# First weights in pieces by pairs of column blocks, and the state of the first batch added on VectorE

## The chip, the cores and the metric

The kernel runs on one core of a Trainium2 chip. A core has a matrix engine (TensorE, PE in the profile, PEld for its weight loads), VectorE (DVE), ScalarE (ACT), GpSimd (POOL) and SyncE (SP), which here issues all transfers. Each engine takes its instructions in the order in which the program gives them. The metric is the device time of one execution in microseconds; the median of three runs is shown.

## The reference

Two stages. The first is an mLSTM cell over 4 batches, 8 heads, 768 steps, head width 40, with a matrix state C per head; the second mixes the result (4 x 768 x 320) by a Fourier transform over tokens and features and puts it through a two-layer MLP with 320 -> 1280 -> 320.

```python
for t in range(S):
    m_new = np.maximum(f_gate[:, :, t] + m, i_gate[:, :, t])
    f_stab = np.exp(f_gate[:, :, t] + m - m_new)
    i_stab = np.exp(i_gate[:, :, t] - m_new)
    C = f_stab[:, :, None, None] * C + i_stab[:, :, None, None] * np.einsum('bhd,bhe->bhde', vt, kt)
    n = f_stab[:, :, None] * n + i_stab[:, :, None] * kt
    h_tilde = np.einsum('bhde,bhe->bhd', C, qt)
    y[:, :, t] = o * h_tilde / denom
...
X = np.real(np.fft.fft(np.fft.fft(x, axis=1), axis=2))
u = x + X
un = (u - mu) / np.sqrt(var + 1e-06)
ch = np.maximum(un @ w_ch1, 0.0) @ w_ch2
return u + ch
```

The weights `w_ch1` and `w_ch2` come as 64-bit floats and are turned into 32-bit floats on the chip.

## The kernel before

**Tiling.** The 768 steps of a batch are 6 chunks of 128 tokens (`NT`). Within a chunk the cell is matrix work: scores q.k (`ps`, L465), weighing by the gates' exponentials (`W`, L421 on ScalarE, L471 on VectorE), the part from the state (`ph<-qg,C`, L479), the part from the chunk itself (`ph<-W,kvt`, L486), and the chunk's contribution to the state (`pc<-vw,kvt`, L496). Then `h` is copied out by ScalarE, transposed (`px`, L535) and divided (L544 to L550, VectorE). Three buffers `C_bufs` hold the state in turn.

**State.** In batches 1 to 3 GpSimd multiplies the old state by its decay into the next buffer (L455), and VectorE adds `pc` to it (L515; a copy, L513, for chunk 0). In batch 0 GpSimd writes the decayed state into a side buffer `Cd`, two multiplications by an identity add it to `pc` on TensorE (L501), and ScalarE copies the sum into the next state (L511).

**Mixing and MLP.** The Fourier stage folds token blocks on VectorE and GpSimd (`mix_fold`), multiplies by tables (`pz`, `pzt`, then `pu`), adds to x (`mix_add`, L743 to L757, VectorE), centres (`uc`, L765, ScalarE), transposes (`put`, L772) and copies out (`uT`, L777, ScalarE). The MLP works on two groups of three token blocks; 1280 hidden columns are 10 blocks, taken as 5 pairs. For batch 0, `mlp_in` (L837 and, for the 64 odd features, L841) gives a pair's two banks, which ScalarE puts through a relu (L850), and `mlp_out` (L943) multiplies by the second weights. For the other batches, `mlp_block` and `mlp_out_pair` use sums of blocks (seven products in place of eight), which `weight_sums`, `mlp_sums`, `hidden_sums` and `out_weight_sums` make on VectorE.

**Weights in pieces.** A `Piece` is 128 x 640 64-bit numbers, 640 KB. It is loaded into one of two `raw` buffers (L334), taken apart by two VectorE instructions (`take`, L344 and L346), converted by two of ScalarE (`convert`, L351 and L352) and joined by three of VectorE (`join`, L358 to L364). The first weights are five pieces: the first half of the columns of features 0 to 127, the same half of the last 128 features, the 64 features between (`w1t_sb`), then the second halves. So a first product needs three pieces. The second weights are five pieces more, one for each pair.

**The order** is written out by hand. `at(slot, phase, fn)` puts a call into a plan, and the plan is run in the order of (slot, phase); that order is the order in each engine's queue. Batch 0 has slots 0 to 21 for its chunks (three slots each), 18 to 31 for the mixing, and 31 on for its MLP, one product step a slot; chunks of batch 1 start at slot 32 and lie between these. `EVAC`, `FILL`, `MAIN`, `FILL_PE` are phases 0 to 3. `when` gives the slots of take, convert and join of each piece, `early` and the loop under it the slots of its load. A load waits for its `raw` buffer to be free, and everything behind it in SyncE's queue waits with it.

Steps in slots 31 to 37 that are spoken of below, in the order of ScalarE's queue: exponentials of batch 1's chunk 0, first half (slot 32), relu of the first pair (33, phase 0), exponentials, second half (33), centring of token block 4 (33), copy of its transpose (34), conversion of the first piece of the second weights (34), relu of the second pair (35). On VectorE: addition for block 4 (31), join of the last first-weight piece (32), taking (33), weighing of chunk 0 (34), addition for block 2 (35), join (35), state copies (36), taking (36), addition for block 3 (37).

## Time and profile before

| | |
|---|---|
| median of three runs | 420.96 us (420.94 to 421.48) |
| the profiled execution | 420.94 us |
| its span, first to last instruction | 419.2 us |
| mean granted TensorE clock | 0.999 |
| bytes moved | 47.14 MB, mean 112 GB/s |
| first products of the MLP of batch 0 | from 58.0 us |
| first products with the second weights | from 122.6 us |

A row of the timeline is: start and duration in us, engine, line of the kernel, operation, output<-inputs, shapes, count, and in brackets the engine's idle time before it with what ended it. Rows of consecutive instructions of one line are merged, so the duration of a row with x4 is that of all four. In the page's second part a digit is the busy share in tenths of one of 40 slices of the span (10.5 us each).

### The profile page before, as it was taken

Reading aid. Unit: us, or ns where it says so; the run is one execution under the profiler, and the core shown is the slowest. Engines: PE = TensorE matmul, PEld = TensorE weight load, DVE = VectorE, ACT = ScalarE, POOL = GpSimd, SP = SyncE. Lnnn points to the kernel's source line nnn. Section 1 sums busy time; section 2 is a strip of 40 time slices with the busy share of each in tenths; the row PEclk is TensorE's granted clock in tenths of the full one; section 3 lists DMA queues with packets and bytes.
Section 4 is the critical chain, followed back from the end, with each engine's and each line's share of the span. In section 5 each row is a group of like instructions: output and inputs, shape, how many; then the busy total and the mean of one; then the engine's idle time right before and its main releaser. Section 6 shows DMA issues by size and latency. Waiting matters only on the chain.

```text
span 419.2 us, 8001 instructions
## 1 busy us (share of the span) xinstructions
PE 408.1 (97%) x2966; PEld 302.4 (72%) x2966; DVE 288.8 (69%) x682; ACT 189.5 (45%) x493; POOL 112.9 (27%) x194
## 2 busy tenths in 40 slices
PE   8999999999999999999999999999999999999997
PEld 6877555566567778776549998976559988455996
DVE  8789895777895638777765569788663786335652
ACT  6986376686561222654455413744451113355000
POOL 5554201468431520442231430351220000020000
PEclk9999999999999999999999999999999999999999
DMA  7899297567765254276100554310000000000010
GB/s 230 288 250 318 71 278 257 185 162 219 236 189 164 59 155 139 64 210 197 50 0 2 156 149 131 100 42 1 0 2 0 33 31 34 0 2 0 16 48 31
DMA packets 20549, 47.14 MB, mean 112 GB/s; under 512 B 2784, under 2 KB 9312, under 8 KB 20384
## 3 DMA queue, kind: packets, MB, share of 16 engines
q1 hardware_dynamic: 20512, 46.65, 36.7%
q8 instruction: 23, 0.38, 0.4%
q14 instruction: 14, 0.11, 0.1%
HBM read 42.52 MB, written 4.11 MB: 111 GB/s over the span
## 4 chain that ended last, share of the span: by engine, by line
PE 82%; DVE 7%; DMA 4%; issue 3%; ACT 2%; POOL 1%; ACTq 0%; DVEq 0%; POOLq 0%; SPq 0%
PE po L999 18%; PE pm L897 17%; PE po L943 8%; PE pm L902 5%; PE ps L465 5%; PE ph L486 4%; PE pu L729 4%; PE ph L479 3%; PE pm L837 3%; DMA raw<-in_w 3%; PE px L535 2%; PE put L772 2%; PE pz L698 2%; DMA kvt<-in_kv 1%; PE pz L686 1%
## 5 line engine op out<-in xcount | busy, mean ns | idle before, releaser
L949 DVE SCALAR_TENSOR_TENSOR x<-po,rstd,x 128x160 f32<-128x160 f32 (+1 forms) x69 | 27.0, 395 | 40.2 <-PE po L999 34.1
L906 DVE TENSOR_TENSOR h<-h,pm 128x384 f32<-128x384 f32 x60 | 30.5, 550 | 30.5 <-ACT h L919 20.9
L421 ACT ACTIVATE W<-W,colT 128x128 f32<-128x128 f32 x144 | 45.0, 395 | 0.0
L443 POOL TENSOR_SCALAR_AFFINE_SELECT W<-W 128x1024 f32<-128x1024 f32 x18 | 21.6, 1198 | 81.0 <-ACT W L421 59.1
L943 PE MATMUL po<-w_sb,h 128*128 128x320 f32 x120 | 34.4, 435 | 0.0
L897 PE MATMUL pm<-uT,w_sb 128*128 128x384 f32 x90 | 32.8, 492 | 0.2 <-DVE uT L885 0.2
L471 DVE TENSOR_TENSOR W<-ps,W 128x512 f32<-128x512 f32 x48 | 30.7, 680 | 2.6 <-POOL W L443 2.4
L837 PE MATMUL pm<-uT,w_sb 128*128 128x384 f32 x80 | 29.6, 499 | 0.7 <-DVE x L749 0.5
L777 ACT COPY uT<-put 128x384 f32<-128x384 f32 x24 | 11.2, 478 | 40.2 <-PE put L772 40.2
L943 PEld LDWEIGHTS po<-w_sb,h 128*128 128x128 f32 x120 | 22.2, 190 | 9.5 <-issue 0.8
L999 PE MATMUL po<-T,S 128*128 128x160 f32 x180 | 27.9, 302 | 0.6 <-DVE x L949 0.6
L465 PE MATMUL ps<-qk 40*128 40x128 f32 x384 | 27.8, 284 | 0.0
L999 PEld LDWEIGHTS po<-T,S 128*128 128x128 f32 x180 | 25.5, 190 | 2.2 <-DVE x L949 1.0
L792 POOL TENSOR_TENSOR t<-rstd 128x6 f32<-128x6 f32 x12 | 2.9, 244 | 89.2 <-DVE v L790 88.6
L999 PE MATMUL po<-w_sb,h 128*128 128x160 f32 x180 | 26.4, 301 | 0.0
L465 PEld LDWEIGHTS ps<-qk 40*128 40x128 f32 x384 | 23.4, 187 | 4.1 <-issue 0.7
L999 PEld LDWEIGHTS po<-w_sb,h 128*128 128x128 f32 x180 | 25.1, 190 | 1.3 <-DVE x L949 0.3
L486 PE MATMUL ph<-W,kvt 128*41 128x128 f32 x384 | 25.8, 277 | 0.0
L431 POOL TENSOR_TENSOR qg<-qk,Gb 128x512 f32<-128x512 f32 x18 | 25.2, 1402 | 0.1
L524 ACT COPY h<-ph 41x512 f32<-41x512 f32 (+1 forms) x16 | 9.3, 583 | 34.9 <-PE ph L486 34.8
L479 PEld LDWEIGHTS ph<-qg,C 128*128 128x128 f32 x160 | 20.0, 191 | 6.3 <-issue 2.5
L897 PEld LDWEIGHTS pm<-uT,w_sb 128*128 128x128 f32 x90 | 16.2, 190 | 10.8 <-DVE h L906 1.5
(207 smaller groups left out, 864.6 us busy)
## 6 DMA issues: line engine op xcount, KB each, us to landing
W<-M_d SPq DMA_DIRECT2D x18, 512.0 KB
kvt<-in_kv SPq DMA_DIRECT2D x24, 324.0 KB
qk<-in_qkT SPq DMA_DIRECT2D x48, 160.0 KB
raw<-in_w SPq DMA_DIRECT2D x10, 640.0 KB
Gb<-G_d SPq DMA_DIRECT2D x36, 128.0 KB
so<-in_o SPq DMA_DIRECT2D x24, 160.0 KB
out<-x SPq DMA_DIRECT2D x24, 160.0 KB
ds_sb<-in_dft_s SPq DMA_DIRECT2D x1, 1155.0 KB
```

Of the source, the lines that this page charges most:

```text
L421: nc.scalar.activation(out=k.W[:, h, :], in_=M, func=AF.Exp, scale=-1.0, bias=colT[:, c, 0, b * H + h:b * H + h + 1])
L431: nc.gpsimd.tensor_tensor(out=k.qg, in0=k.qk[:, 0], in1=k.Gb, op=OP.mult)
L465: nc.tensor.matmul(k.ps[hip][:, p, :], k.qk[r, 1, p, :], k.qk[r, 0, p, :], start=True, stop=True)
L471: nc.vector.tensor_tensor(out=Wv, in0=k.ps[hip], in1=Wv, op=OP.mult)
L479: nc.tensor.matmul(k.ph[:, p, :], k.C[:, p, :], k.qg[:, p, :], start=(p == 0), stop=False, skip_group_check=True)
L486: nc.tensor.matmul(k.ph[hip * 64:hip * 64 + D1, p, :], k.v1[:, 2 * p + hip, :], k.W[:, 2 * p + hip, :], start=(c == 0 and p == 0), stop=Tr ...
L837: nc.tensor.matmul(k.pm[i], w1_sb[:, ch, f0:f0 + L], u[2 * ch], start=(ch == 0), stop=False)
L897: nc.tensor.matmul(bank, w, u, start=start, stop=True, skip_group_check=True)
L906: nc.vector.tensor_tensor(out=h, in0=h, in1=bank, op=OP.add)
L943: nc.tensor.matmul(k.po, hidden(gr, f)[:, i * L:(i + 1) * L], w2_sb[:, f, :], start=(f == 0), stop=(f == NFF - 1))
L949: nc.vector.scalar_tensor_tensor(out=u, in0=po, scalar=k.rstd[:, c:c + 1], in1=u, op0=OP.mult, op1=OP.add)
L999: nc.tensor.matmul(po, a[:, f], w[:, f], start=start and f == 0, stop=f == half - 1, skip_group_check=True)
```

## The change

It has two parts, and two small ones that follow from them.

- The first weights lie in `w1_sb` as five groups, one for each pair of column blocks, of five 128-column blocks: features 0 to 127 for either block of the pair, the last 128 features for either, and the 64 features between. One piece is one group. `w1t_sb` is gone; the host packs the array accordingly, and the products and weight sums read the new places.
- The slots of the pieces change: the second piece is loaded at slot 6 and converted in slots 11 to 22, and so on; the last piece of the first weights has slots 31, 32 and 33, and the pieces of the second weights start one slot later.
- In batch 0 the state is handled as in the other batches: GpSimd writes the decayed state into the next buffer, VectorE adds `pc` (or copies it, chunk 0). The identity multiplications and ScalarE's copies are gone, and so are the `Cd` buffers and their clearing.
- The name of the change also speaks of sums for the first pair of token blocks; the diff has no line on `hidden_sums` or its slots.

```diff
+    w1_sb = const.tile([L, NFF // 2, 5, L], FP, name="w1_sb")
-    w1_sb = const.tile([L, 2, DFF], FP, name="w1_sb")
-    w1t_sb = const.tile([L, DFF // 2], FP, name="w1t_sb")
...
         mlstm_load(0, 2)
-        w1_pieces[1].load()
-        for t in hT_bufs + Cd_bufs:
+        for t in hT_bufs:
             nc.gpsimd.memset(t, 0.0)
...
-    w1_pieces = [Piece([w1_sb[:, f // 2, f % 2 * part:(f % 2 + 1) * part]], w_ch1[:, f * part:(f + 1) * part])
-                 for f in (0, 2, 1, 3)]
-    w1_pieces.insert(2, Piece([w1t_sb], w_ch1[:, 4 * part:]))
+    w1_pieces = [Piece([w1_sb[:, i].rearrange("p k t -> p (k t)")], w_ch1[:, i * 5 * L:(i + 1) * 5 * L])
+                 for i in range(NFF // 2)]
...
-                nc.gpsimd.tensor_tensor(out=k.Cd[r] if b == 0 else k.C_next[r, :, m], in0=k.C[r, :, m], in1=d,
-                                        op=OP.mult)
+                nc.gpsimd.tensor_tensor(out=k.C_next[r, :, m], in0=k.C[r, :, m], in1=d, op=OP.mult)
...
-            if add:
-                for hip in range(2):
-                    r = slice(hip * 64, hip * 64 + D)
-                    nc.tensor.matmul(k.pc[r], ident[:, r], k.Cd, start=False, stop=True, skip_group_check=True)
...
-                if b == 0:
-                    nc.scalar.copy(out=Cv, in_=k.pc[r])
-                elif c == 0:
+                if c == 0:
                     nc.vector.tensor_copy(out=Cv, in_=k.pc[r])
                 else:
                     nc.vector.tensor_tensor(out=Cv, in0=Cv, in1=k.pc[r], op=OP.add)
...
-            nc.tensor.matmul(k.pm[i], w1_sb[:, ch, f0:f0 + L], u[2 * ch], start=(ch == 0), stop=False)
+            nc.tensor.matmul(k.pm[i], w1_sb[:, f // 2, 2 * ch + i], u[2 * ch], start=(ch == 0), stop=False)
...
-    when = [((2, 0.7), (4, 0.5), (6, 0.6)), ((6, 0.7), (7, 0.5), (8, 0.6)), ((11, 0.7), (13, 0.5), (22, 0.6))]
-    when += [((22, 0.7), (23, 0.7), (27, 0.6)), ((27, 0.7), (28, 0.7), (32, 0.6))]
-    when += [((s, 0.7), (s + 1, 0.7), (s + 2, 0.6)) for s in (33, 36, 39, 42, 45)]
+    when = [((2, 0.7), (4, 0.5), (6, 0.6)), ((11, 0.7), (13, 0.5), (22, 0.6)), ((22, 0.7), (23, 0.7), (27, 0.6)),
+            ((27, 0.7), (28, 0.7), (31, 0.6))]
+    when += [((s, 0.7), (s + 1, 0.7), (s + 2, 0.6)) for s in (31, 34, 37, 40, 43, 46)]
     pieces = w1_pieces + w2_pieces
     for n, (w, p) in enumerate(zip(when, pieces)):
-        if n > 4:
+        if n > 3:
             at(when[n - 2][2][0] + 1, FILL + 0.7, p.load)
...
-             (5, mlstm_load_decay, 4), (6, None, 2), (7, mlstm_load_o, 3), (7, mlstm_load, 5),
-             (11, mlstm_load_decay, 5), (11, None, 3), (11, mlstm_load_o, 4), (12, load_tables, None),
-             (14, mlstm_load_o, 5), (23, None, 4)]
+             (5, mlstm_load_decay, 4), (6, None, 1), (7, mlstm_load_o, 3), (7, mlstm_load, 5),
+             (11, mlstm_load_decay, 5), (11, None, 2), (11, mlstm_load_o, 4), (12, load_tables, None),
+             (14, mlstm_load_o, 5), (23, None, 3)]
```

## The prediction

> **What bounds the kernel now.** I read the page first (busy shares, then the slices), then the chain of waits, then the timeline of each engine from 0 to 130 us, where all that the change touches lies, and last the busy time by windows around the one long wait found there. The page:

> ```profile
> PE 408.1 (97%) x2966; PEld 302.4 (72%) x2966; DVE 288.8 (69%) x682; ACT 189.5 (45%) x493; POOL 112.9 (27%) x194
> DMA  7899297567765254276100554310000000000010
> ```

> TensorE is busy for 97% of the span, so what it is made to wait anywhere is paid in full, and other work counts only where TensorE comes to wait for it. The transfers fill the first 120 us and are thin after that. The first batch, up to 58 us, from the timelines of TensorE, ScalarE and VectorE (start, duration, instruction, count, idle time before it and its releaser):

> ```profile
> 15.77 0.60 ACT L511 COPY C<-pc 40x164 f32<-40x164 f32 x2 [0.19 <-PE pc L496]
> 16.14 0.44 PE L297 MATMUL pd<-dec,spread_sb 32*128 32x80 f32 x2 [0.42 <-DVE dec L293]
> 21.91 0.45 PE L501 MATMUL pc<-s_last,ident 128*40 128x164 f32 x4
> 22.41 0.62 ACT L511 COPY C<-pc 40x164 f32<-40x164 f32 x2 [0.80 <-PE pc L501]
> 23.76 0.66 PE L535 MATMUL px<-ident,h 128*128 128x128 f32 x4 [0.41 <-ACT h L528]
> 39.00 1.28 DVE L471 TENSOR_TENSOR W<-ps,W 128x512 f32<-128x512 f32 x2
> 39.35 0.61 ACT L511 COPY C<-pc 40x164 f32<-40x164 f32 x2 [0.63 <-PE pc L501]
> 40.07 1.13 PE L479 MATMUL ph<-qg,C 128*128 128x128 f32 x8 [0.82 <-POOL eo L618]
> ```

> The state C of each chunk goes through ScalarE; at 40.07 TensorE waits for it (the copies end at 39.96, which fits better than the releaser named). VectorE is full from 24.8 to 41.3 us and has only 0.33 us of idle time up to 51.8. Then the first MLP. Same columns, from SyncE's, ScalarE's, VectorE's and TensorE's timelines, and one line by windows (busy time of the engines, granted clock, DMA share, GB/s):

> ```profile
> 59.91 0.53 SPq L334 DMA_DIRECT2D raw<-in_w  x1
> 60.35 1.26 ACT L421 ACTIVATE W<-W,colT 128x128 f32<-128x128 f32 x4
> 61.72 0.87 ACT L850 ACTIVATE h<-pm 128x384 f32<-128x384 f32 x2
> 62.48 1.27 ACT L421 ACTIVATE W<-W,colT 128x128 f32<-128x128 f32 x4
> 63.65 0.61 ACT L765 ACTIVATE uc<-x 128x384 f32<-128x384 f32 x1
> 64.56 0.49 PE L772 MATMUL put<-ident,uc 128*128 128x128 f32 x3
> 67.83 0.49 DVE L344 TENSOR_SCALAR e<-raw 128x640 uint32<-128x640 uint32 x1 [5.02 <-DMA raw<-in_w]
> 68.35 0.83 ACT L351 ACTIVATE e<-e,ebias 128x640 uint32<-128x640 uint32 x1 [2.79 <-DVE e L344]
> 73.60 0.69 DVE L513 COPY C<-pc 40x164 f32<-40x164 f32 x2 [0.23 <-PE pc L496]
> 76.58 2.82 PE L837 MATMUL pm<-uT,w_sb 128*128 128x384 f32 x8 [0.52 <-DVE x L749]
> 64.00:66.00 2.00, 2.00 (x10) 1.06 (x10) 0.00 (x0) 0.73 (x2) 1.62 (x2) 1.00 1.07 284
> ```

> The weight piece asked for at 59.91 lands only at 67.8, behind saturated transfers (share 1.00 to 1.07 from 58 to 68 us). VectorE waits 5.02 us for it; ScalarE reaches its conversion with all of TensorE's near work (relu, exponentials, centring for the transpose at 64.56) already done, so nothing is lost. That order is what the change turns round.

> **The change, part by part.** All sums are made in the profiled execution: 420.94 us, of which 419.2 is the span; the median shown is 420.96.

> *Layout of the first weights and of its sums.* The same matmuls, tails and four weight sums of 128x640 read other offsets; nothing. The words "sums for the first pair of token blocks" have no line in the diff; nothing.

> *State of the first batch.* Gone are 16 identity matmuls (21.91 to the next at 22.30, so 0.39 us per chunk, four chunks, 1.6 us), ten copies on ScalarE (0.30 each) and two small memsets on GpSimd, 0.23 each, hidden beside the gate scans. The decay on GpSimd writes the next state instead of the side buffer, same shape and count (0.46). Added on VectorE are ten instructions, priced by the later batches' rows of the same form, 0.69 us a pair for a copy (L513) and 0.68 for an add (L515). What is queued behind them decides:
> - Chunk 0: VectorE now has to wait for pc (15.72) and copy C (15.77 to 16.45) before qg (L429, 0.60) and dec (0.2). dec ends at 17.3, so pd, which started at 16.14, starts at 17.3: +1.15 us on TensorE.
> - Chunks 1 to 3: per chunk TensorE saves those 0.39 us and, for two of them, the 0.41 wait for h, which ScalarE now copies first. So +1.15 becomes +0.15 at the state product of chunk 2 (one wait more is used up by C), -0.8 at chunk 3 and -1.2 at chunk 4.
> - VectorE, meanwhile, can't use the early piece that was taken out of slots 6 to 8 (0.9 taking, 3.3 joining): the add of chunk 2 stands before the weighing of chunk 3 and waits for pc at about 27.9, so that weighing starts at 28.6 instead of 28.16, +0.45. From there its queue is full as before, with one add before the weighing of chunk 4 (0.68; the taking of a piece at 31.0, 1.45 beside GpSimd's qg, may be 0.3 shorter: +0.85 altogether) and one behind the weighing of chunk 5 (0.67). C of chunk 5 is ready at 39.00 + 0.85 + 1.28 - 0.08 + 0.67 = 41.7 us, and TensorE's state product starts at 41.72 instead of 40.07.
> Result: **+1.65 us** at the end of the first batch, because the folds and divisions behind it are on VectorE as well. From both sides: -2.4 (1.6 of matmuls and two waits of 0.4, if VectorE has the room) and +2.5 (1.15 + 0.69 + 0.67, if nothing is won back). I take the walk through the queues.

> *The pieces of the first weights.* Before, five pieces were converted in slots 2-6, 6-8, 11-22, 22-27 and 27-32. After: 2-6, 11-22, 22-27, 27-31, 31-33. The load of 640 KB at 7.95 us goes; the next three keep their places in SyncE's queue with other contents. The fifth piece is asked for where the first piece of the second weights was, at slot 28, into a buffer free at 57.5, behind the same loads: 59.91, landed at 67.8. But its conversion stands at slot 32, ahead of relu, exponentials and centring. So ScalarE, done with the first four exponentials at 61.6, stands until VectorE has taken the piece, and converts from 68.35 to 69.8. Queued behind it: two relu, four exponentials and the centring of token block 4, which take 63.65 - 61.72 = 1.93 to reach the centring, from 69.72. That starts at 71.65 and ends at 72.26; the transpose on TensorE follows at 72.3 instead of 64.56. TensorE is done with the two products ahead of it at 64.65, and all behind the transpose waits in order: **+7.65 us**. The bounds are 6.5 (a landing 1.2 us sooner, as 655 KB less went before at 280 GB/s would save half of 2.3) and 8.5 (0.85 for the relu again, if the exponentials behind them wait). What the cover was worth: the same 5.02 us wait cost nothing while only the second weights hung on it.

> *The second weights, one slot later.* Joining the first of their pieces moves from before the state copies at 73.60 to between these and block 3's addition (L743 to L757), where only a taking of 0.93 stood. The join is 0.79 + 0.82 + 0.83 with overlaps, 2.35. TensorE's product at 76.58 waits for L749 already (0.52 idle), so 2.35 - 0.93 = **+1.4 us**; bounds 0, if VectorE is ahead after the stall, and 2.3, when GpSimd's work makes it longer as at 24.82 (1.83 for 0.8). The waits for weights at 96 and 106 us move behind the weighings: from -0.8 (idle 0.23 and 0.61 gone) to +0.8 (a join of 2.4 in the place of a take and a wait of 1.15), I take 0.

> *The clock after an idle TensorE.* No idle time over 1.25 us is in this trace, and the granted clock is 1.00 in every window, so no row prices a gap of 7.6. Nearest is the start, where the first six idle products took 2.93 us, against 0.60 for two at 54.96: 2.93 - 3 x 0.60 = 1.1 us of slow products. From below 0 (below nothing makes no sense, for a product can't become faster than at full clock), from above 2.9, if all that stretch's time is added. I take **+1.1**, by the row it is nearest to.
> [...]

> Sum: 420.94 + 1.65 + 7.65 + 1.4 + 1.1 = **432.7 us**.

> **Rivals.**
> - *No stall, and the first batch gains.* It decides at one point: does the fifth piece land before ScalarE is through the exponentials at 61.6? Then 420.94 - 2.4 = 418.5, faster. For it: the transfers' share is 0.21 from 42 to 48 us and one early load is gone. Against: from the asking to 61.6 are 1.7 us, where the same place in the queue took 7.9.
> - *The stall, but a shorter first batch.* VectorE squeezes the adds into its gaps: -2.4 + 7.65 + 1.4 gives 427.6. For it: four waits of 0.4 to 0.8 on TensorE before 44 us hang on ScalarE, which is relieved. Against: VectorE has no gap from 24.8 on.
> - *No stall, but VectorE the bound of the first batch:* 1.65 + 1.4, 424.0. The same landing decides.
> - *The change doesn't do what it says:* for the sums of the first pair this holds, and it gives the forecast's time.

> **How the numbers follow.** Forecast 0.62, stall with a shorter first batch 0.24, no stall but a loss 0.07, no stall and a gain 0.07. The forecast's own range is 429.5 to 436.5 (clock and stall at their ends); for 8 in 10 I reach down to 427.3, which takes in most of the second case. Within 0.2%, 0.84 us, is about what can't be told from no change: faster 0.06, same 0.02, slower 0.92.

> **What would show it.** ScalarE's first conversion line (L351 before) after 60 us should have an idle time of about 6.7 us before it, and TensorE's next transpose one of about 7.6 after ScalarE's centring, with a granted clock under 1.00 in the next slice if the clock falls. The state product of chunk 5 should start near 41.7, pd near 17.3, and the first MLP product near 59.6. The prediction falls if the fifth piece is taken before 63, or if that transpose has no wait.

## The result, and the profile after

The changed kernel takes 442.73 us (median of 4 runs, 441.49 to 445.02) against 421.22 us (4 runs, 420.94 to 422.31) for the kernel before in the same comparison: a ratio of 1.051 [1.046, 1.057], some 21.5 us slower. The forecast was 432.7 with a range to 436.5, so the direction held and the size did not. The profiled execution took 445.02 us, the slowest of the four, with a span of 443.3 us, 24.1 more than before; the sums below are made in it.

First the page of the kernel after: busy times, and the granted clock by slices.

```profile
PE 417.7 (94%) x2950; PEld 309.2 (70%) x2950; DVE 290.5 (66%) x692; ACT 186.6 (42%) x483; POOL 113.3 (26%) x192
PEclk9898997779998999999999999999999999999999
```

TensorE is busy for 9.6 us longer than before (408.1) with 16 matmuls fewer, and its clock, 9 in every slice before, dips in six slices, all in the first 145 us. So there are two kinds of loss to look for: time in which TensorE stands, and time in which it runs slowly. The timeline of TensorE has both (start, duration, instruction, idle time before it and its releaser):

```profile
16.88 0.45 PE L294 MATMUL pd<-dec,spread_sb 32*128 32x80 f32 x2 [1.67 <-DVE dec L290]
20.15 1.85 PE L471 MATMUL ph<-qg,C 128*128 128x128 f32 x8
43.40 1.13 PE L471 MATMUL ph<-qg,C 128*128 128x128 f32 x8 [0.94 <-DVE C L500]
61.34 2.85 PE L821 MATMUL pm<-uT,w_sb 128*128 128x384 f32 x8
76.83 0.90 PE L757 MATMUL put<-ident,uc 128*128 128x128 f32 x3 [8.77 <-ACT uc L750]
80.52 2.51 PE L714 MATMUL pu<-dd_sb,Z 128*128 128x321 f32 x4
84.22 2.20 PE L821 MATMUL pm<-uT,w_sb 128*128 128x384 f32 x6
94.14 5.46 PE L821 MATMUL pm<-uT,w_sb 128*128 128x384 f32 x8 [2.79 <-DVE x L734]
120.67 1.16 PE L471 MATMUL ph<-qg,C 128*128 128x128 f32 x8 [0.97 <-POOL qg L426]
132.46 1.13 PE L471 MATMUL ph<-qg,C 128*128 128x128 f32 x8 [1.60 <-DVE x L535]
146.69 3.50 PE L927 MATMUL po<-w_sb,h 128*128 128x320 f32 x12
```

The row at 76.83 is the stall that was foretold: the transpose of token block 4 waits 8.77 us for ScalarE's centring. The rows behind it show what was not foretold in its size: the same four products of `pu` take 2.51 us at 80.52, where they took 1.35, and the eight of `pm` at 94.14 take 5.46 in place of 2.82. The same rows in the kernel before (those at 64.56 and 76.58 stand in the prediction):

```profile
58.00 2.85 PE L837 MATMUL pm<-uT,w_sb 128*128 128x384 f32 x8
66.47 1.35 PE L729 MATMUL pu<-dd_sb,Z 128*128 128x321 f32 x4
68.93 2.22 PE L837 MATMUL pm<-uT,w_sb 128*128 128x384 f32 x6
99.44 1.16 PE L479 MATMUL ph<-qg,C 128*128 128x128 f32 x8 [0.23 <-POOL qg L431]
110.20 1.13 PE L479 MATMUL ph<-qg,C 128*128 128x128 f32 x8 [0.61 <-DVE den L544]
122.60 5.65 PE L943 MATMUL po<-w_sb,h 128*128 128x320 f32 x20
```

Laid side by side, stretch by stretch:

| TensorE, from and to | before | after | more |
|---|---|---|---|
| start to the first MLP product | 58.00 | 61.34 | 3.34 |
| to the transpose of block 4 | 6.56 | 15.49 | 8.93 |
| to the products behind `pu` (84.22) | 4.37 | 7.39 | 3.02 |
| to the products that wait for block 3's addition (94.14) | 7.65 | 9.92 | 2.27 |
| to the state product at 120.67 | 22.86 | 26.53 | 3.67 |
| to the state product at 132.46 | 10.76 | 11.79 | 1.03 |
| to the first product with the second weights | 12.40 | 14.23 | 1.83 |
| to the end of the span | 296.6 | 296.6 | 0.0 |

The sum is 24.1 us: all of it is lost before the second weights are used. The cause of the stall stands in the timelines of SyncE, VectorE and ScalarE:

```profile
63.60 0.53 SPq L331 DMA_DIRECT2D raw<-in_w  x1
72.37 0.49 DVE L341 TENSOR_SCALAR e<-raw 128x640 uint32<-128x640 uint32 x1 [6.23 <-DMA raw<-in_w]
72.90 0.83 ACT L348 ACTIVATE e<-e,ebias 128x640 uint32<-128x640 uint32 x1 [7.95 <-DVE e L341]
74.26 0.85 ACT L834 ACTIVATE h<-pm 128x384 f32<-128x384 f32 x2
75.00 1.27 ACT L416 ACTIVATE W<-W,colT 128x128 f32<-128x128 f32 x4
76.17 0.61 ACT L750 ACTIVATE uc<-x 128x384 f32<-128x384 f32 x1
```

The fifth piece is asked for at 63.60 and taken at 72.37. ScalarE stands 7.95 us in front of its conversion, and the relu, the exponentials and the centring (76.17), for which the data had long been there, come only after it. The windows (busy time of TensorE, weight load, VectorE, ScalarE and GpSimd, then the granted clock, DMA share, GB/s) tell when the clock fell and rose again:

```profile
18.00:20.00 2.00, 2.00 (x21) 1.71 (x19) 0.80 (x2) 1.98 (x9) 1.64 (x6) 0.56 0.82 270
20.00:22.00 2.00, 2.00 (x13) 1.73 (x10) 1.68 (x3) 0.21 (x1) 0.00 (x0) 0.59 1.00 211
...
72.00:74.00 2.00, 0.00 (x0) 0.00 (x0) 1.14 (x3) 1.10 (x2) 0.00 (x0) 0.71 0.32 130
...
80.00:82.00 2.00, 2.00 (x5) 1.08 (x4) 0.00 (x0) 1.38 (x5) 0.00 (x0) 0.50 0.70 194
82.00:84.00 2.00, 2.00 (x8) 1.00 (x7) 0.00 (x0) 2.00 (x6) 0.00 (x0) 0.73 0.04 8
```

From about 72.8 to 83.1 the array ran at half its clock (0.50 in each window of 2 us from 74 to 82), more than six microseconds of that with TensorE at work. The same shows from 93.3 to 100.1 (0.50 from 94 to 100), and for 3.4 us each at 18.2, 38.7 and 134.3 (0.50 in windows that lie within them: 18.5 to 21.5, 40 to 42, 134.5 to 137.5).

### The profile page after: what moved, and what is told of

Read it like the earlier page. It is cut to its first block, busy times and chain, and to the rows that moved or that the text cites. A ratio compares the mean times of both kernels' runs of the same rounds, so it can differ in the third digit from the quotient of the medians.

```text
span 443.3 us, 7963 instructions
## 1 busy us (share of the span) xinstructions
PE 417.7 (94%) x2950; PEld 309.2 (70%) x2950; DVE 290.5 (66%) x692; ACT 186.6 (42%) x483; POOL 113.3 (26%) x192
## 4 chain that ended last, share of the span: by engine, by line
PE 80%; DVE 12%; ACT 2%; DMA 2%; issue 2%; POOL 2%; ACTq 0%; DVEq 0%; POOLq 0%
PE po L983 17%; PE pm L881 16%; PE po L927 7%; PE pm L886 5%; PE ph L478 5%; PE ps L457 5%; PE ph L471 4%; PE pu L714 4%; PE pm L821 3%; DMA raw<-in_w 2%; PE put L757 2%; PE px L520 2%; PE pz L683 2%; PE pc L487 1%; PE pz L671 1%
## 5 line engine op out<-in xcount | busy, mean ns | idle before, releaser
L438 POOL TENSOR_SCALAR_AFFINE_SELECT W<-W 128x1024 f32<-128x1024 f32 x18 | 21.5, 1192 | 98.3 <-ACT W L416 74.3
L821 PE MATMUL pm<-uT,w_sb 128*128 128x384 f32 x80 | 33.1, 547 | 2.9 <-DVE x L734 2.8
L881 PE MATMUL pm<-uT,w_sb 128*128 128x384 f32 x90 | 32.8, 492 | 0.2 <-DVE uT L869 0.2
L457 PE MATMUL ps<-qk 40*128 40x128 f32 x384 | 28.8, 286 | 0.6 <-PE pM L215 0.4
L983 PE MATMUL po<-T,S 128*128 128x160 f32 x180 | 27.9, 302 | 0.6 <-DVE x L933 0.6
L457 PEld LDWEIGHTS ps<-qk 40*128 40x128 f32 x384 | 24.1, 189 | 4.9 <-issue 1.6
L478 PE MATMUL ph<-W,kvt 128*41 128x128 f32 x384 | 27.5, 289 | 0.0
L471 PEld LDWEIGHTS ph<-qg,C 128*128 128x128 f32 x160 | 21.2, 202 | 8.2 <-issue 3.9
L500 DVE TENSOR_TENSOR C<-C,pc 40x164 f32<-40x164 f32 x32 | 10.3, 322 | 25.3 <-PE pc L487 23.3
L471 PE MATMUL ph<-qg,C 128*128 128x128 f32 x160 | 23.1, 291 | 3.5 <-DVE x L535 1.6
```

The costliest lines, as they stand in the source:

```text
L457: nc.tensor.matmul(k.ps[hip][:, p, :], k.qk[r, 1, p, :], k.qk[r, 0, p, :], start=True, stop=True)
L471: nc.tensor.matmul(k.ph[:, p, :], k.C[:, p, :], k.qg[:, p, :], start=(p == 0), stop=False, skip_group_check=True)
L478: nc.tensor.matmul(k.ph[hip * 64:hip * 64 + D1, p, :], k.v1[:, 2 * p + hip, :], k.W[:, 2 * p + hip, :], start=(c == 0 and p == 0), stop=Tr ...
L821: nc.tensor.matmul(k.pm[i], w1_sb[:, f // 2, 2 * ch + i], u[2 * ch], start=(ch == 0), stop=False)
L881: nc.tensor.matmul(bank, w, u, start=start, stop=True, skip_group_check=True)
L983: nc.tensor.matmul(po, a[:, f], w[:, f], start=start and f == 0, stop=f == half - 1, skip_group_check=True)
```

## The experiments

Two theories stood at the start. **The order**: the fifth piece's conversion stands ahead of ScalarE's near work, and all else follows from that wait. **The layout, the transfers or the state**: the new pieces, or VectorE's additions, cost the time in themselves. Each kernel was timed against the kernel before on the same chip. The table has one profile of each as well: `pm - ps` is the time from the scores of chunk 0 to the first MLP product, which leaves out the start (the scores began between 6.89 and 9.64 us in these profiles). The last column lists the stretches at half clock up to 150 us, as start and length. A stretch's length is worked out from windows of 2 us: the sum of (1 - clock) x 2 x 2 us, for a window that lies wholly in a stretch shows a clock of 0.50. A profile is of one run: those of x9, x10 and x11 are of the slowest run of their kernel (428.88, 428.93 and 426.90 us), that of x8 of the fastest.

| kernel | median us | ratio to before | pm - ps | half clock: start (length) |
|---|---|---|---|---|
| before | 421.22 | | 50.45 | none |
| after | 442.73 | 1.051 [1.046, 1.057] | 54.30 | 18.2 (3.4), 38.7 (3.4), 72.8 (10.2), 93.3 (6.8), 134.3 (3.4) |
| x1_fifth_later | 425.30 | 1.009 [1.006, 1.012] | 52.70 | 37.7 (3.4) |
| x2_state_alone | 426.92 | 1.013 [1.008, 1.018] | 54.93 | 43.9 (3.4) |
| x3_pieces_alone | 440.54 | 1.042 [1.037, 1.048] | 50.45 | 68.0 (10.2), 88.5 (6.8), 129.4 (3.4) |
| x7_pieces_later | 422.62 | 1.001 [1.000, 1.003] | 50.36 | none |
| x6_filled_18 | 440.04 | 1.042 [1.041, 1.044] | 52.62 | 37.8 (3.4), 89.0 (6.8), 130.0 (3.4) |
| x4_filled | 448.92 | 1.063 [1.055, 1.071] | 54.34 | 18.3 (3.4), 38.8 (3.4), 96.8 (6.8), 137.8 (3.4) |
| x8_own_buffer | 436.24 | 1.033 [1.031, 1.035] | 54.32 | 18.5 (3.4), 39.0 (3.4) |
| x5_qg_first | 425.74 | 1.009 [1.007, 1.011] | 51.13 | 37.7 (3.4) |
| x9_take_sooner | 425.66 | 1.010 [1.007, 1.013] | 55.04 | 45.0 (3.4) |
| x10_sooner_qg_first | 425.35 | 1.008 [1.006, 1.010] | 56.31 | 31.4 (6.8), 45.0 (3.4) |
| x11_early_load | 423.91 | 1.004 [1.002, 1.006] | 51.23 | 35.5 (3.4), 114.0 (6.8) |
| x12_order | 427.40 | 1.012 [1.009, 1.014] | 52.62 | 41.6 (6.8), 109.9 (3.4) |

### The pieces at their old places in the queues

```diff
-    when += [((s, 0.7), (s + 1, 0.7), (s + 2, 0.6)) for s in (31, 34, 37, 40, 43, 46)]
+    when += [((s, 0.7), (s + 1, 0.7), (s + 2, 0.6)) for s in (33, 36, 39, 42, 45, 48)]
```

> The changed kernel, but the fifth piece of the first weights is taken, converted and joined in slots 33, 34 and 35, behind the relu and the centring of token block 4, and the second weights in slots 36 to 50. Theory 'order in ScalarE's queue': the wait of 8.77 us at the transpose goes, and with it the 2.79 us wait at the following pair and the slow clock behind both, so 424 us, which is before plus the 3.3 us by which the first batch ends later (423 to 426). Rival 'state': the loss is that of the first batch and of a clock that falls there and does not recover; then this stays above 432 us.

From 1.051 to 1.009: the places in the queues, of the fifth piece and of those of the second weights, and nothing else, are worth 18 of the 21.5 us ((1.0512 - 1.0087) x 421.2). The transpose of block 4 has no wait in this profile, and the clock does not fall behind it; ScalarE still waits for the piece, but behind its centring (rows of ScalarE and TensorE):

```profile
66.44 0.60 ACT L750 ACTIVATE uc<-x 128x384 f32<-128x384 f32 x1
67.34 0.49 PE L757 MATMUL put<-ident,uc 128*128 128x128 f32 x3
71.07 0.83 ACT L348 ACTIVATE e<-e,ebias 128x640 uint32<-128x640 uint32 x1 [2.71 <-DVE e L341]
```

That settles the order as the main cause.

### One part of the change at a time

`x2_state_alone` is the kernel before with the state added by VectorE; `x3_pieces_alone` is the change with the old way of the state (identity matmuls, ScalarE's copies).

> The kernel before with only the state of the first batch moved to VectorE; pieces and slots as before. Theory 'order in ScalarE's queue': the first product of the MLP starts 1.7 to 3.5 us later, nothing else moves, 422.5 to 424.5 us. Rival 'state': above 430 us.

> The changed kernel with the state of the first batch as before (identity products on TensorE, copies on ScalarE). Theory 'order in ScalarE's queue': the transpose waits 8 to 9 us as in the changed kernel, the clock falls behind it; the first batch ends at 58 us or up to 2 us sooner, as a piece is out of its VectorE queue; 436 to 440 us. Rival 'state': below 430 us.

The pieces alone give 440.54, the state alone 426.92, both more than expected: 19.1 and 5.5 us over the 421.43 of their comparison, more together than the 21.5 of the whole change, so the parts do not simply add up. In x2's profile the product of chunk 5's state waits 2.15 us for VectorE's addition, where it waited 0.82:

```profile
43.30 1.47 PE L475 MATMUL ph<-qg,C 128*128 128x128 f32 x8 [2.15 <-DVE C L504]
```

Last, x3 with the edit of x1:

> The pieces by pairs alone (state as before), with the fifth in slots 33 to 35. Theory 'order in ScalarE's queue': with the conversion behind the centring nothing is left of the loss, 420.5 to 422 us, the same as before. Rival 'a piece more among the first products costs by itself' (VectorE 3.4 us, ScalarE 1.5 us, a slot later for the second weights): 424 us or more.

422.62 against 422.10, 1.001 [1.000, 1.003]. So the layout, the packing and the later asking for the second piece cost nothing that can be measured. What x1 still loses is the state's.

### Idle time or clock: the stall filled with products

A row of idle products, whose output nothing reads, is put into TensorE's queue ahead of the transpose of block 4; they fill the wait without shortening it. The fill was meant for about 8 us.

```diff
+    def idle_more(n):
+        pw = ps_h.tile([L, 2 * L], FP, name="pi", tag="ph")
+        for i in range(n):
+            nc.tensor.matmul(pw, rest[:, 0:L], rest, start=True, stop=True, skip_group_check=True)
+
+    at(33, FILL_PE + 4.9, idle_more, 36)
```

> The changed kernel with 36 products of zeros put on TensorE ahead of the transpose that waits, about 7.7 us of work that nothing reads. If the idle time itself costs clock: the transpose starts at the same time or at most 0.5 us later, the granted clock stays at 1.00 from 68 to 84 us and the products behind it take their full-clock times, so 438 to 440 us, 3 us less than the changed kernel. If the low clock has another cause: 442 to 444 us, and the clock still falls near 73 us.

One call is two instructions in the trace and takes 0.44 us, so 36 of them took 15.7 us, twice what was meant, and the transpose was late by them (83.50). The time of this run says little; its clock says more, 1.00 in every window from 68 to 96. With 18 calls the fill ends where the wait did:

> The changed kernel with 18 products of zeros ahead of the waiting transpose, half of x4's, 7.8 us. Idle time costs clock: the transpose starts within 0.3 us of the time at which ScalarE has centred, the clock stays at 1.00 up to the next gap, the stretch from the transpose to the additions of block 2 takes 4.4 us in place of 7.4, so 438 to 440.5 us. If not: 442 to 444 us.

Two rows of x6's timeline, the fill and the transpose behind it, and the next gap:

```profile
67.33 7.93 PE L1108 MATMUL pi<-rest 128*128 128x256 f32 x36
75.39 0.55 PE L757 MATMUL put<-ident,uc 128*128 128x128 f32 x3
...
89.74 5.46 PE L821 MATMUL pm<-uT,w_sb 128*128 128x384 f32 x8 [2.80 <-DVE x L734]
```

From the transpose to the products behind `pu` it is 4.43 us (75.39 to 79.82), nearly as before the change (4.37), against 7.39 in the kernel after. So the wait itself costs its length, and its being idle costs 3.0 us more; the ratio goes from 1.051 to 1.042, with intervals that do not meet. Behind the unfilled gap of 2.80 at 89.74 the clock still halves (0.50 in the windows from 90 to 94): 5.46 in place of 2.82.

### Landing or place in the queue: a buffer of its own for the fifth piece

The order of the change is kept, but the fifth piece is loaded at slot 23 into a free part of the hidden layer's buffer.

```diff
-            self.raw = cp.tile([L, n], mybir.dt.int64, name="raw", tag="raw")
+            if self is w1_pieces[4]:
+                self.raw = hid[1, 1][:, 0:2 * n].bitcast(mybir.dt.int64)
+            else:
+                self.raw = cp.tile([L, n], mybir.dt.int64, name="raw", tag="raw")
...
-            at(when[n - 2][2][0] + 1, FILL + 0.7, p.load)
+            at(*((23, FILL + 0.9) if n == 4 else (when[n - 2][2][0] + 1, FILL + 0.7)), p.load)
```

> The changed kernel, order of the engines' queues unchanged, but the fifth piece has a buffer of its own and is asked for at slot 23, right behind the fourth. If the landing is what ScalarE's order turns into a stall: the conversion at slot 32 finds it landed (before 62 us), the transpose waits under 1 us, and what stays is the first batch (3.3) and the join ahead of block 3's addition (1.4 to 2.3): 425.5 to 427.5 us. If the place in the queue costs by itself: above 432 us.

A miss: 436.24 (the profile is of the fastest run, 432.51). VectorE takes the piece with no wait for its transfer, but TensorE still waits, as its timeline shows:

```profile
70.78 0.55 PE L760 MATMUL put<-ident,uc 128*128 128x128 f32 x3 [2.57 <-ACT uc L753]
...
85.13 2.82 PE L824 MATMUL pm<-uT,w_sb 128*128 128x384 f32 x8 [2.80 <-DVE x L737]
```

Of the 8.77 us of the stall 6.2 were the landing; 2.57 remain, for the taking stands behind VectorE's join of the fourth piece (63.90 to 66.3) and the conversion behind the taking, still ahead of the centring. The waits of the second weights' pieces are as in the kernel after: 2.80 here, later 0.98 and 1.61. In this profile, unlike the others, the gap of 2.80 left the clock alone (1.00 in every window from 82 to 100, 2.82 for the same eight products). The other four runs took 435.65 to 436.68 at a mean granted clock of 0.980 to 0.984, against 0.992 in this one, so they ran at the low clock for longer; where, no trace shows. So taking the transfer away mends two thirds of the wait; the order mends all of it.

### What the state on VectorE costs

Five kernels stand on x1. In `x5_qg_first` the scaled query of chunk 1 and the decays go ahead of the first copy of the state.

```diff
-        at(4, FILL + 0.5, decays)
+        at(4, FILL - 0.1, decays)
...
-            at(s if (b, c) == (0, 2) else s + 1, FILL + 0.1, mlstm_scale_q, b, c)
+            at(s if (b, c) == (0, 2) else s + 1, FILL + (-0.2 if (b, c) == (0, 1) else 0.1), mlstm_scale_q, b, c)
```

> The fifth piece later, as in x1, and in chunk 0 VectorE does qg and dec ahead of the copy of the state, as their order was before. If the wait of 1.68 us at pd is paid in full: 423.6 us, 1.7 less than x1 (423.0 to 424.3), with pd waiting 0.4 us. Rival 'VectorE is the bound of the first batch from 25 us on': the wait is swallowed there, 425 us, within 0.5 of x1.

The wait of `pd` is gone and `pm - ps` is 1.57 us shorter than in x1, but the time is the same. This profile's scores began 1.55 us later than x1's (9.64). The edit alone does not bring that about, for with the same edit they begin at 8.34, 7.13 and 8.34 in x10, x11 and x12; how the median can keep none of the gain is not settled. The next kernels look behind chunk 1. In x1, VectorE has 2.73 us with nothing to do ahead of the addition for chunk 2, then a full queue, and the scores of chunk 5 come to wait:

```profile
35.22 1.72 PE L457 MATMUL ps<-qk 40*128 40x128 f32 x16 [0.45 <-PE pM L215]
37.48 0.91 PE L520 MATMUL px<-ident,h 128*128 128x128 f32 x4 [0.54 <-ACT W L416]
...
42.85 1.13 PE L471 MATMUL ph<-qg,C 128*128 128x128 f32 x8 [0.95 <-DVE C L500]
```

So the second piece is taken apart in that free time (slot 9 and 10 in place of 11 and 13), without and with x5's edit:

> x1_fifth_later (425.3 us) with the second piece taken apart at slot 9 and converted at slot 10, in place of slots 11 and 13. In x1 VectorE stands idle for 2.73 us before the addition to the state of chunk 2 (25.96 to 28.69) and then has a full queue, in which the taking (0.80) stands ahead of the weighing of chunk 4; the scores of chunk 5 on TensorE wait for that weighing, and its clock falls there (products of chunk 4 take 1.91 and 1.58 in place of 1.06 and 1.07). Theory (the price of the state on VectorE is the length of VectorE's queue at chunk 4): the weighing of chunk 4 starts 0.8 us sooner, the scores of chunk 5 wait 0.5 less, the clock stays up if the gap was what lowered it; first MLP product 1.0 to 2.5 us sooner than x1's 60.79, time 422.8 to 424.5. Rival (the price is the wait of the first chunk and the latency from pc to C, wherever the taking stands): 425 to 425.6.

> x9_take_sooner with the scaled query of chunk 1 and the decays ahead of the first copy of the state on VectorE, as in x5_qg_first. Theory (with the queue at chunk 4 shortened, the start of chunk 1 is what is late, and what is won there is kept): 0.8 to 1.2 us under x9, 421.5 to 423.5, near the kernel before. Rival (as in x5, nothing is won by it): as x9 to 0.4 us.

Both miss the theory, at 425.66 and 425.35. In the profiles, which are of the slowest runs, the piece had not landed: VectorE waits 3.88 us for it in x9 and 4.23 in x10, and TensorE 1.5 and 1.8 at the state product of chunk 3. How late it was in the runs near the median is not shown. With the piece loaded at the start, where the kernel before loads one, the same orders give:

> x10_sooner_qg_first with the second piece loaded at the start, where the kernel before loads a piece, in place of slot 6. In x9 and x10 that piece, taken apart at slot 9, landed only at 28.9 to 29.8, and TensorE waited 1.5 to 1.8 us at the state product of chunk 3; the start of chunk 1 in x10 was 1.26 us sooner than in x9 (state product 19.02 to 20.28). Theory (the price of the state on VectorE is what VectorE is late by, at the first copy and from chunk 3 on; with the piece there in time, its 2.73 idle us take it up): no wait at the state product of chunk 3, the weighing of chunk 4 before 33.5, the first MLP product 57.5 to 59.0, and the time 420.5 to 422.5, the rest of it the waits for pieces of the second weights near 110 us. Rival (the additions on VectorE cost their latency in every chunk, wherever the rest stands): 424 to 425.5.

423.91, 1.004 [1.002, 1.006]: less than half of x1's loss is left, though not the 422.5 or less that was expected. From the timeline of x11's slowest run:

```profile
35.56 1.92 PE L472 MATMUL ph<-qg,C 128*128 128x128 f32 x8
37.40 1.77 PE L479 MATMUL ph<-W,kvt 128*41 128x128 f32 x16
...
113.07 1.23 PE L472 MATMUL ph<-qg,C 128*128 128x128 f32 x8 [2.64 <-DVE den L530]
```

`pm - ps` is 0.78 us longer than before. One stretch at half clock, on these two rows, costs 1.6 of that (1.92 and 1.77 in place of 1.06 and 1.07): without it the first batch would, by this sum, be some 0.8 us shorter than before, which no run tests. The wait at 113 is another matter: the pieces of the second weights are three slots later than before, and VectorE stands 2.32 us for one of them (taken at 109.15) ahead of a weighing and the divisions behind it, on one of which (L530) TensorE's wait ends (it waited 0.61 there before). A last kernel tried both: the addition for chunk 3 behind the weighing of chunk 4, and slots 32, 35 and so on for the pieces.

> x11_early_load (423.9 us) with two orders mended. First, the addition to the state of chunk 3 behind the weighing of chunk 4 on VectorE: in x11 the weighing starts at 32.06, though its exponentials are there at 30.6, and the scores of chunk 5 and the transposition at 35.05 wait 0.25 and 0.48 us, behind which the granted clock fell to 0.50 (products of chunk 4 1.92 and 1.77 in place of 1.06 and 1.07). Second, the fifth piece of the first weights and all pieces of the second one slot sooner (32 and on, in place of 33), the conversion still behind the centring of token block 4: in x11 VectorE is late with a piece of the second weights near 110 us, and TensorE waits 2.64 us for it at the state product of chunk 4 of batch 1 (0.61 before). Theory (both are the rest of the price): weighing of chunk 4 at 30.8 to 31.2, the state product of chunk 5 0.5 to 2.5 us sooner, the wait near 110 us under 1.5; time 421 to 422.8, no loss against the kernel before. Rival (the clock falls there whatever the small gaps are, and the late pieces are set by the transfers): 423.5 to 424.5.

A clear miss, 427.40. The scores of chunk 5 no longer wait, but the lateness moves to the state of chunk 5, and two products `pc` near 97 and 109 us wait 1.00 and 2.04, which have no wait in x11:

```profile
40.28 1.13 PE L472 MATMUL ph<-qg,C 128*128 128x128 f32 x8 [2.12 <-DVE C L499]
```

What each of the two orders costs alone is not shown. No version here is faster than the kernel before. What x11's remaining 0.4% is stays open: its three fastest runs, 422.62 to 422.91 us at a mean granted clock of 0.996 to 1.000, lie near the median of 422.39 of the kernel before, and the slowest, 426.90 at 0.987, is the one profiled.

## Why the prediction was wrong

Point by point, by its steps, in the profiled execution:

- **Layout: nothing.** Right (x7, 1.001).
- **The stall, +7.65, bounds 6.5 and 8.5.** Right in place and cause, a little small: 8.77. The piece was taken 8.77 us after it was asked for, where the row copied from before gave 7.9.
- **The join ahead of block 3's addition, +1.4, bounds 0 and 2.3.** The mechanism holds; the wait went from 0.52 to 2.79, so 2.27, the upper end. The last instruction of the join took 1.59 beside GpSimd's work, not 0.82.
- **The second weights' pieces one slot later, taken as 0.** Wrong by 1.7: the waits at 120.67 and 132.46 grew by 0.74 and 0.99.
- **State of the first batch, +1.65.** `pd` was late by 1.25 (forecast 1.15), the wait for C came where it was expected, but the stretch is 3.34 longer (3.85 from the first scores). The walk through the queues counted TensorE's products at full clock; two half-clock stretches of 3.4 us (granted clock 0.50) lie in it in this profile, which at the most cost half their length each, 3.4 together.
- **The clock after an idle TensorE, +1.1, bounds 0 and 2.9.** This is the step that failed. It was priced from the slow start, for one gap, and by its words "no row prices a gap of 7.6"; the row it took is not one at a low clock either, for the granted clock of the kernel before is 1.00 in the windows from 0 to 4 us. What the runs put in its place: 3.0 us behind the 8.8 us gap (x6 takes this away), and 4.5 more behind smaller gaps, which the forecast itself had named and priced at their length alone: 2.9 behind the 2.79 at 94.14 (3.67 less the longer wait of 0.74), and 1.55 of the 1.83 behind the 1.60 at 132.46. No run fills these two gaps; in x1, where TensorE waits 0.53 and 1.37 at the same places, the clock does not fall there. With the first batch's two stretches the clock took 7.5 to 11 of the 24.1 us.
- **The range, 429.5 to 436.5, "clock and stall at their ends".** These ends give 430.5 to 435.4; with those of the join as well it is 429.1 to 436.3.

Forecast terms against what this profile has: first batch 1.65 and 3.34, stall 7.65 and 8.93, join 1.4 and 2.27, later pieces 0 and 1.7, clock 1.1 and 7.5 outside the first batch (3.02, 2.93 and 1.55). The rivals without a stall fell with the 8.77 us; "a shorter first batch" fell with x2. That the sums of the first pair would not show was right, and of no weight.

## What to carry to other kernels

In an in-order queue the place of an instruction that waits for a transfer must be behind all work that is ready sooner and that the bounding engine needs; here the fifth piece and those behind it, two slots earlier, cost 18 us more (x1). Price a gap of TensorE not by its length alone: add what the clock does behind it, here 3.0 us behind the gap of 8.77 and 2.9 behind that of 2.79, but nothing behind the 2.80 in x8's profile. Exchanging two instructions of an engine that is full for a stretch won nothing here (x12, which changed one thing more); what helped was work brought forward into its idle time, and only once the transfer for it had been brought forward too (x10 against x11, 1.008 and 1.004).

## What the runs showed of the hardware

**The same gap does not always lower the clock.** The wait of `pd`, 1.67 us in the kernel after and 1.68 in x1, was followed by 0.56 and 0.59 in the windows from 18 to 22 in the one and by 1.00 in the other:

```profile
18.00:20.00 2.00, 2.00 (x26) 1.57 (x28) 1.44 (x3) 1.98 (x6) 1.15 (x3) 1.00 0.22 63
```

(x1, same columns.) In the kernel after, the gap from 15.21 to 16.88 lies inside one step of 3.413 us, counted back from the fall (14.83 to 18.24); the clock falls at that step's end. In x4 and x8 as well the gap of 1.68 lies inside one step, and the clock falls at its end (18.28 and 18.48); in x1, x2, x6 and x9 a step, counted back in the same way from the later fall, ends within the gap (at 17.20, 16.61, 17.36 and 17.65), and the clock stays at 1.00. That is a reading of seven profiles, not shown as a rule: a step in which TensorE was busy for 0.74 of the time by the profile was followed by a fall (x11, from 32.07), one with 0.43 was not (x9, from 113.23), so the idle share alone does not decide it, and what else does stays open. For measuring: these kernels spread by 1 to 7 us between runs (x3 took 436.18 at a mean clock of 0.988 and 440.44 to 440.89 at 0.977), where the kernel before, with no gap over 1.25 us, stays within 1 to 3.
